# Fused attention and two MoE layers on one core: scores, turning and tails issued in another order, and a four-operation weight decoder

## The chip, the cores and the metric

The kernel runs on one core of a Trainium2 chip. The metric is the device time of one execution in microseconds (us). The engines named here are TensorE (PE in the rows, its weight loads PEld), VectorE (DVE), ScalarE (ACT), GpSimd (POOL) and the queue on SyncE that issues the transfers (SP).

## What is computed

The reference chains three layers over 4 x 576 tokens of width 512:

```python
scores = scale * np.matmul(q, k.transpose(0, 1, 3, 2)) + bias      # 4 batches, 8 heads, 576 x 576
scores = scores - np.max(scores, axis=-1, keepdims=True)
attn = np.exp(scores)
attn = attn / (np.sum(attn, axis=-1, keepdims=True) + 1e-09)
x = matmul(attn, v)                                                # heads joined: 2304 x 512
h = np.maximum(np.maximum(x @ w1, x @ w2), x @ w3)                 # width 768
y = h @ w_out
g = elu(y @ w_in)                                                  # width 2048
out = g @ w_out2
```

The bias depends on the distance of two positions and comes from a small two-layer net. The weights of the two MoE layers come as 64-bit floats.

## The kernel before

**Stages.** From 0 to about 62 us the bias of all heads is computed and written to a scratch array in DRAM. Then comes the attention, up to about 404 us; then the first MoE layer, up to about 713 us, and the second to the end.

**Steps of the attention.** It is cut into 80 steps: 16 groups (one batch and two heads) of five steps, called c0 to c4 here. A step handles 128 query rows of both heads; the last, c4, has 64 rows of both heads in one tile. For step s the program issues:

- *queries times keys* (`unit_qk`, L222): TensorE writes the products of head 0 into the PSUM tile pb0 and those of head 1 into pb1 (c4: pb0 alone).
- *scores* (L230): VectorE adds the bias, writes the tile `e_t` and finds the row's minimum, once for each head. ScalarE then takes the exponential (L235) with the row's sum.
- *reciprocal* (L240, L241) and *diagonal* (L249): one step later VectorE inverts the sums and GpSimd spreads them into a diagonal matrix `dg_t`.
- *turning* (`trans`, L252): two steps later TensorE multiplies `e_t` by that diagonal, which transposes and scales it, into the PSUM tiles tq0 and tq1. `evac` (L295) copies both to SBUF, tq0 by ScalarE, tq1 by VectorE where the step's number is in `EVD` and by ScalarE otherwise.
- *tails* (`tails`, also L252): the last 64 keys are turned into columns of pb0 that the scores don't use (64 to 127 and 832 to 895; the scores use 224 to 799). `evac_tails` (L306) copies them to SBUF with VectorE.
- *values* (`pv`, L319 to L327): TensorE multiplies the turned weights by v into xo0 and xo1. Twice in a group the result is copied out by ScalarE (`x_copy`), summed by VectorE (`x_sum`, L345) and split into a high and a low part by GpSimd.

**What sets the order.** There is no scheduler: every call is entered with a number, the plan is sorted by it, and each engine runs its calls in that order. The numbers are the step plus an offset from the table `OFF`. A call is made to wait for earlier calls on the same PSUM tile; of two calls on pb0 the one that is entered later waits for the one entered sooner.

**Decoder.** Beside the attention, and then beside the first MoE layer, a generator (`decoder`) turns 64-bit weights into 32-bit ones, tile by tile (56 tiles). Each `pump` runs it to its next `yield`. In the attention one pump follows in four of five steps, and a tile takes five pumps. A tile's five VectorE operations stand at L420, L423, L425, L427 and L430, and one ScalarE operation at L422. `split` then makes high and low parts on ScalarE and GpSimd. `fetch` loads the raw tile after the next.

Of the kernel before, what the change touches and what calls it, by code (L numbers as in the profile page):

```python
# [11 lines left out]
F32 = mybir.dt.float32  # L12
F32R = mybir.dt.float32r
I32 = mybir.dt.int32
AF = mybir.ActivationFunctionType
ALU = mybir.AluOpType
# [11 lines left out]
NU = NF // 2  # L28
NB = 384
BIG = 3.0e38  # L30

OFF = {"qk0": 0.0, "qk1": 0.01, "t0": 0.30, "t1": 0.31, "pump": 0.32, "ns": 1.305, "dg": 1.306, "tr": 2.10, "tl": 2.20,
       "evt": 2.311, "ev0": 2.385, "ev1": 2.387, "ex0": 0.38, "ex1": 0.40}
PV_AT = {1: [(4.5, 0), (4.5, 1), (5.5, 2), (5.5, 3), (5.5, 4)],
         4: [(3.5, 0), (3.5, 1), (4.5, 2), (4.5, 3), (5.5, 4)]}
X_AT = {1: 5.6, 4: 5.6}
EVD = {0, 1, 2}  # L40

MOE_LD = 74.39
MOE_AT = [(79.60, 81.00), (80.60, 81.45), (82.00, None)]
# [10 lines left out]
def fused_kernel(ctx, tc, tkq, vv, lt, pk, wm1, wo1, win2, wo2, out):  # L54
    nc = tc.nc
    mm = nc.tensor.matmul

    const = ctx.enter_context(tc.tile_pool(name="const", bufs=1))
# [3 lines left out]
    wpre = wst.enter_context(tc.tile_pool(name="wpre", bufs=1))  # L62

    ident = const.tile([128, 128], F32, name="ident")
    make_identity(nc, ident)
    rebias = const.tile([128, 1], F32, name="rebias")
    nc.vector.memset(rebias, -896.0 * 2.0 ** 23)

    scr = [dram.tile([128 if c < 4 else 64, H, S], F32, name=f"scr{c}") for c in range(5)]

    def hi_of(eng, dst, src):
        if eng == "p":
            nc.gpsimd.tensor_scalar(dst, src, 1.0, 1.0, op0=ALU.mult, op1=ALU.mult)
        elif eng == "a":
            nc.scalar.activation(dst, src, AF.Copy)  # L75
        else:
            nc.vector.tensor_copy(dst, src)  # L77
# [43 lines left out]
    with ExitStack() as pro:  # L121
# [18 lines left out]
        with tc.manual_schedule():  # L140
# [38 lines left out]
            for A in range(36):  # L179
# [15 lines left out]
                c, r = divmod(A, 8)  # L195
# [29 lines left out]
    def scores(s, h):  # L225
        n, c = steps[s]
        if h == 0:
            E[s] = ep.tile([128, 1152], F32, tag="e", name="e_t")
            ST[s] = sp.tile([128, 8], F32, tag="st", name="st_t")
        nc.vector.tensor_tensor_reduce(out=E[s][:, 576 * h:576 * h + 576], in0=PB[h][:, 224:800], in1=BT[n // 4, c, h],  # L230
                                       op0=ALU.add, op1=ALU.min, scale=-0.125, scalar=BIG, accum_out=ST[s][:, h:h + 1])

# [57 lines left out]
    def evac(s, g):  # L290
        n, c = steps[s]
        p = PT[n, c > 1][0]
        if c < 4:
            q0 = 128 * (c % 2) + 64 * g
            hi_of("v" if g and c in EVD else "a", p[:, :, q0:q0 + 64], TQ[g].rearrange("p (k q) -> p k q", k=8))  # L295
        else:
# [58 lines left out]
    DQ = []  # L355
# [4 lines left out]
    RAW = {}  # L360
    n_raw = [0]

    def fetch():
        if n_raw[0] >= len(DQ):
            return
        key = DQ[n_raw[0]]
        n_raw[0] += 1
        r = wpre.tile([128, 512, 2], I32, tag="raw", name="raw", bufs=2)
        src = {"w1": lambda: wm1[key[1], key[2]], "wo": lambda: wo1[key[1]], "wi": lambda: win2[key[1] + NU * key[2]],
               "w3": lambda: wo2[key[1] + NU * key[2]]}[key[0]]()  # L370
        nc.sync.dma_start(r.rearrange("p n t -> p (n t)"), src.bitcast(I32))
        RAW[key] = r
# [7 lines left out]
    def split(key, src, c0=0):  # L380
        direct = key[0] == "w1" and 3 * key[1] + key[2] == WN[0] and WN[0] < WN[1] + 6
        if key[0] == "wo":
            sp2 = WO[0][:, key[1]]
        elif direct:
            sp2 = wr.tile([128, 2, 512], F32R, tag="w", name="w_t")
            WS.append((key, sp2))
            WN[0] += 1
            HERE.add(key)
        else:
            pool, tag = (WPRE2[0], "sp3") if WPRE2 and NSP[0] % 3 == 2 else (wpre, "sp2")  # L390
            sp2 = pool.tile([128, 2, 512], F32R, tag=tag, name=tag, bufs=2 if tag == "sp2" else 1)
            NSP[0] += bool(WPRE2)
        hi, lo, src = sp2[:, 0, c0:], sp2[:, 1, c0:], src[:, c0:]
        parts = [partial(hi_of, "a", hi, src), partial(lo_of, "p", lo, src, hi)]
        if key[0] != "wo":
            parts.append(partial(todo.append, (key, sp2, c0)))
        else:
            SCW[key] = None
        if lim[0] < len(DQ):
            late.extend([parts[0:1], parts[1:3], [store]])  # L400
        else:
            for fn in parts:
                fn()

    def decoder():
        for i, key in enumerate(DQ):
            while i >= lim[0]:
                yield
            if key[0] != "wi":
                dst = wpre.tile([128, 512], F32, tag="t", name="t_w", bufs=2)  # L410
            elif key[2]:
                cw = WPRE2[0].tile([128, 4, 512], F32, tag="cw", name="cw_t", bufs=1)
                dst = cw[:, 3]
            else:
                dst = cw[:, 0]
            t = dst.bitcast(I32)
            r = RAW.pop(key)
            lo, hi = r[:, :, 0], r[:, :, 1]
            x = wpre.tile([128, 512], I32, tag="x", name="x_t", bufs=2)
            nc.vector.tensor_scalar(x, hi, 0x7FF00000, None, op0=ALU.bitwise_and)  # L420
            yield
            nc.scalar.activation(x, x, AF.Relu, bias=rebias, scale=8.0)  # L422
            nc.vector.tensor_scalar(t, hi, 3, 0x7FFFF8, op0=ALU.logical_shift_left, op1=ALU.bitwise_and)  # L423
            yield
            nc.vector.scalar_tensor_tensor(out=t, in0=hi, scalar=-0x80000000, in1=t, op0=ALU.bitwise_and, op1=ALU.bitwise_or)  # L425
            yield
            nc.vector.scalar_tensor_tensor(out=t, in0=lo, scalar=29, in1=t, op0=ALU.logical_shift_right, op1=ALU.bitwise_or)  # L427
            yield
            fetch()
            nc.vector.tensor_tensor(out=t, in0=t, in1=x, op=ALU.bitwise_or)  # L430
            if key[0] != "wi":
                split(key, dst)
            elif key[2] == 0:

                a11, a12, a21, a22 = (cw[:, p, c:c + 256] for p in (0, 3) for c in (0, 256))
                s2, s1, s3, s4 = (cw[:, p, c:c + 256] for p in (1, 2) for c in (0, 256))
                for d, a, b, op in ((s1, a21, a22, ALU.add), (s2, s1, a11, ALU.subtract), (s3, a11, a21, ALU.subtract),
                                    (s4, a12, s2, ALU.subtract)):
                    yield
                    nc.vector.tensor_tensor(out=d, in0=a, in1=b, op=op)  # L440
                for p in range(4):
                    yield
                    if p:
                        yield
                    split(("wi", key[1], p), cw[:, p], 256 if p == 3 and key[1] > 1 else 0)
                    if len(todo) > 1:
                        store()
            yield
            if len(todo) > 1:
                store()  # L450
        while todo:
            store()
# [8 lines left out]
    def store():  # L461
        if not todo:
            return
        key, sp2, c0 = todo.pop(0)
        d = dram.tile([128, 2, 512], F32, name=f"scw_{key[0]}_{key[1]}_{key[2]}")
        nc.sync.dma_start(d[:, :, c0:], sp2.bitcast(F32)[:, :, c0:])
        SCW[key] = d

    dec = decoder()

    def pump(k=1):
# [76 lines left out]
    def at(key, fn, *args):  # L548
        plan.append((key, len(plan), fn, args))

    for s, (n, c) in enumerate(steps):
        o = {nm: s + off for nm, off in OFF.items()}
        at(o["qk0"], unit_qk, s, 0)
        at(o["t0"], scores, s, 0)
        at(o["ex0"], expo, s, 0)
        if c < 4:
            at(o["qk1"], unit_qk, s, 1)
            at(o["t1"], scores, s, 1)
            at(o["ex1"], expo, s, 1)
        at(o["ns"], recip, s)  # L560
        at(o["dg"], diag, s)
        at(o["tr"], trans, s)
        at(o["tl"], tails, s)
        at(o["ev0"], evac, s, 0)
        at(o["ev1"], evac, s, 1)
        at(o["evt"], evac_tails, s)
        if c in (1, 4):
            for off, k in PV_AT[c]:
                at(s + off + 0.01 * k, pv, s, k)
            at(s + X_AT[c], x_copy, s)  # L570
            at(s + X_AT[c] + 0.25, x_sum, s)
            at(s + X_AT[c] + 0.5, x_hi, s)
            at(s + X_AT[c] + 0.75, x_lo, s)
        if s > 5 and c != 1:
            at(o["pump"], pump)
        if n % 4 == 3 and n < 15:
            at(s + 0.45, load_b, n // 4 + 1, c)
# [121 lines left out]
    def small(tag, bufs):  # L699
        return mp.tile([128, NB], F32, tag=tag, name=f"{tag}_t", bufs=bufs)  # L700
# [61 lines left out]
    with tc.manual_schedule():  # L762
        for n, u in enumerate(units + [None]):
# [6 lines left out]
            if n < 2:  # L770

                for i in range(2):
                    w = take_w(("wi", u[1], 3 * i))
                    v = take_w(("w3", pre[1], i)) if pre else None
                    for q, (b, d) in enumerate(((B11, B21), (B12, B22))):
# [3 lines left out]
                        c = small("c", 4)  # L779
# [121 lines left out]
```

## Time and profile before

| | us |
|---|---|
| median of 3 runs (lowest, highest) | 1097.67 (1095.53, 1098.22) |
| the profiled execution's own time | 1097.02 |
| its span, from the first to the last instruction | 1095.2 |
| TensorE busy in the span | 989.3 |
| VectorE busy | 708.7 |
| ScalarE busy | 517.6 |
| GpSimd busy | 339.3 |

The span leaves out 1.8 us of the execution's time. TensorE is busy for 90% of the span, but not evenly: the attention is the stage in which it isn't. The granted TensorE clock was 0.992 of full speed on average.

### The profile page before, as it was taken

What the parts mean: (1) busy time and instruction counts of PE and PEld (TensorE: products, weight loads), DVE (VectorE), ACT (ScalarE), POOL (GpSimd) and SP (SyncE); (2) the same over time, 40 slices, a digit from 0 to 9 for tenths busy, and PEclk for the clock granted to TensorE, in tenths of its full rate; (3) what the DMA queues carried; (4) which work ended last, traced back from release to release, by engine and by line L of the source; (5) the groups of instructions that cost most, each with busy time, mean ns of one, the idle gap of its engine ahead of it and who ended that gap; (6) DMA issues with size and microseconds to landing.
All of it is one profiled execution on the core that took longest, in us unless ns stands there. A gap on an engine that the chain in (4) does not pass through costs nothing.

```text
span 1095.2 us, 28524 instructions
## 1 busy us (share of the span) xinstructions
PE 989.3 (90%) x11748; PEld 846.2 (77%) x11748; DVE 708.7 (65%) x1444; ACT 517.6 (47%) x1071; POOL 339.3 (31%) x419
## 2 busy tenths in 40 slices
PE   7967777777777679999999999999999999999998
PEld 3445555555455468999999999998999889988997
DVE  7946676667666665998878698174567436663333
ACT  8935555555555553333343334163445344444433
POOL 0002323223322233444345345122332323232212
PEclk9979999999999999999999999999999999999999
DMA  7731443343352213567798788325556655575553
GB/s 274 280 122 67 139 144 116 127 142 118 108 172 86 86 58 129 194 221 286 257 350 307 247 293 323 117 97 174 178 192 210 237 176 194 193 253 180 188 194 110
DMA packets 65905, 201.00 MB, mean 184 GB/s; under 512 B 7024, under 2 KB 14832, under 8 KB 65776
## 3 DMA queue, kind: packets, MB, share of 16 engines
q1 hardware_dynamic: 65776, 199.18, 53.0%
q8 instruction: 93, 1.52, 0.5%
q14 instruction: 36, 0.29, 0.1%
HBM read 150.78 MB, written 48.37 MB: 182 GB/s over the span
## 4 chain that ended last, share of the span: by engine, by line
PE 80%; DVE 16%; issue 2%; DMA 1%; ACT 0%; SPq 0%; POOL 0%; DVEq 0%; POOLq 0%; ACTq 0%
PE xo L696 16%; PE pb L740 12%; PE pb L526 11%; DVE e_t L230 9%; PE tq L252 7%; PE tq L740 6%; PE pb L222 5%; PE xo L526 5%; PE tq L526 5%; PE pb L620 3%; DVE p L77 3%; PE pb L183 2%; PE pbb L183 2%; PE xo L620 2%; PE tq L620 2%
## 5 line engine op out<-in xcount | busy, mean ns | idle before, releaser
L81 POOL TENSOR_TENSOR gl<-t_t,gh 128x384 fp32r<-128x384 f32 x96 | 108.8, 1144 | 286.0 <-ACT gh L75 286.0
L235 ACT ACTIVATE e_t<-e_t,st_t 128x576 f32<-128x576 f32 x144 | 111.1, 772 | 164.1 <-DVE st_t L240 155.2
L230 DVE CUSTOM_DVE_ANT_0 e_t<-pb,b_t 128x576 f32<-128x576 f32 x144 | 107.7, 748 | 88.3 <-PE pb L252 67.5
L222 PE MATMUL pb<-kq_t 64*64 64x288 f32 x1152 | 90.9, 425 | 74.0 <-DVE p L77 72.8
L249 POOL TENSOR_SCALAR dg_t<-ident,st_t 128x64 f32<-128x64 f32 x144 | 49.8, 359 | 264.3 <-DVE st_t L241 192.1
L222 PEld LDWEIGHTS pb<-kq_t 64*64 64x64 f32 x1152 | 36.5, 134 | 120.9 <-DVE p L77 105.8
L252 PEld LDWEIGHTS tq<-dg_t,e_t 64*64 64x64 f32 x4608 | 91.0, 139 | 41.0 <-DVE p L77 17.1
L740 PE MATMUL pb<-w_t,gh 128*128 128x512 f32 x384 | 119.3, 392 | 0.0
L526 PE MATMUL pb<-xh,w_t 128*128 128x384 f32 x448 | 116.9, 336 | 0.0
L252 PE MATMUL tq<-dg_t,e_t 64*64 64x64 f32 x4608 | 96.4, 225 | 18.5 <-DVE p L77 12.5
L696 PE MATMUL xo<-tt,w_t 128*128 128x384 f32 x528 | 107.4, 338 | 0.0
L696 PEld LDWEIGHTS xo<-tt,w_t 128*128 128x128 f32 x528 | 95.0, 188 | 7.5
L718 ACT ACTIVATE t_t<-c_t 128x384 f32<-128x384 f32 x96 | 50.0, 521 | 103.7 <-DVE c_t L709 95.5
L696 PE MATMUL xo<-xh,w_t 128*128 128x384 f32 x328 | 94.6, 335 | 0.0
L526 PEld LDWEIGHTS pb<-xh,w_t 128*128 128x128 f32 x448 | 81.2, 188 | 0.5 <-issue 0.4
L319 PE MATMUL xo<-p,tv_t 64*64 64x320 f32 (+1 forms) x1024 | 78.7, 408 | 0.9 <-issue 0.5
L740 PEld LDWEIGHTS pb<-w_t,gh 128*128 128x128 f32 x384 | 70.5, 188 | 6.6
L740 PE MATMUL pb<-w_t,gl 128*128 128x512 f32 x192 | 75.5, 393 | 0.0
L526 PE MATMUL pb<-xl,w_t 128*128 128x384 f32 x224 | 75.3, 336 | 0.0
L75 ACT ACTIVATE gh<-t_t 128x384 fp32r<-128x384 f32 x96 | 48.5, 519 | 33.4 <-DVE t_t L726 33.4
L696 PEld LDWEIGHTS xo<-xh,w_t 128*128 128x128 f32 x328 | 60.2, 188 | 3.0
L726 DVE SCALAR_TENSOR_TENSOR t_t<-t_t,c_t 128x384 f32<-128x384 f32 x96 | 59.0, 632 | 4.5 <-ACT t_t L719 4.1
(131 smaller groups left out, 2198.8 us busy)
## 6 DMA issues: line engine op xcount, KB each, us to landing
w_t<-scw_w SPq DMA_DIRECT2D x90, 512.0 KB, 4.4
w_t<-scw_wi SPq DMA_DIRECT2D x74, 512.0 KB, 3.6
kq_t<-tkq SPq DMA_DIRECT2D x16, 864.0 KB, 5.2
scw_wi<-sp SPq DMA_DIRECT2D x26, 512.0 KB, 4.7
scw_w<-sp SPq DMA_DIRECT2D x22, 512.0 KB, 5.3
raw<-wo SPq DMA_DIRECT2D x22, 512.0 KB, 3.8
scr<-o_t SPq DMA_DIRECT2D x36, 288.0 KB, 3.9
raw<-wm SPq DMA_DIRECT2D x18, 512.0 KB, 3.9
```

The source lines that it names most:

```text
L81: e.tensor_tensor(out=dst, in0=src, in1=hi.bitcast(F32), op=ALU.subtract)
L222: mm(PB[h][H64[g], 224 + 288 * r:512 + 288 * r], t[H64[r], 576 + 576 * a + q0:640 + 576 * a + q0], t[H64[r], 288 * a:288 * a + 288], start ...
L230: nc.vector.tensor_tensor_reduce(out=E[s][:, 576 * h:576 * h + 576], in0=PB[h][:, 224:800], in1=BT[n // 4, c, h], op0=ALU.add, op1=ALU.min ...
L235: nc.scalar.activation(e, e, AF.Exp, bias=st[:, h:h + 1], scale=-1.0, accum_out=st[:, 2 + h:3 + h])
L252: mm(dst, E[s][H64[g], k0:k0 + 64], DG[s][H64[g], h % nheads(s)], start=True, stop=True)
L319: mm(XO[g][H64[h], 0:w], v[H64[g], 128 * k + 64 * h:128 * k + 64 * h + 64], ps[0][H64[g], 4 * h + k, :], start=(k == 0), stop=(k == 3 and ...
L526: mm(ps[blk][:, 0:NB], wt[:, ks], xt[:, kk, t0:t0 + NB], start=(j == 0), stop=(j == 11))
L620: mm(ps[blk][:, 0:NB], WO[0][:, kk, wt, ms], xt[:, bs], start=(j == 0), stop=(j == 3 * NM1 - 1))
L696: mm(ps, w[wt][:, ks], b[xt][:, kk], start=(start and j == 0), stop=(stop and j == 5), skip_group_check=True)
L718: nc.scalar.activation(t, c, AF.Relu, scale=-1.0)
L726: pend.append([lambda: nc.vector.scalar_tensor_tensor(out=t, in0=t, scalar=-1.0, in1=c, op0=ALU.add, op1=ALU.max), last])
L740: mm(acc[t], g[:, ts], w[k], start=(f == 0 and i == 0 and j == 0), stop=(f == NU - 1 and i == 1 and j == 2))
```

## The change

Four edits. The offsets of the scores (`t0`, `t1`), of the reciprocal (`ns`) and of the diagonal (`dg`) put the scores of a step ahead of the turning and the tails that share the step, instead of behind them. `x_sum` is entered later, which puts it behind the first scores of the following step. Step c1 leaves `EVD`, so that the copy of its tq1 is ScalarE's. The decoder takes the magnitude of the high word with one ScalarE operation a tile ahead, clamps it, and needs four VectorE operations in place of five.

```diff
-OFF = {"qk0": 0.0, "qk1": 0.01, "t0": 0.30, "t1": 0.31, "pump": 0.32, "ns": 1.305, "dg": 1.306, "tr": 2.10, "tl": 2.20,
-       "evt": 2.311, "ev0": 2.385, "ev1": 2.387, "ex0": 0.38, "ex1": 0.40}
+LEAST, MOST = (float(np.array(b, np.uint32).view(np.float32)) for b in (896 << 20, 0x47EFFFFF))
+OFF = {"qk0": 0.0, "qk1": 0.01, "t0": 0.02, "ns": 1.025, "dg": 1.026, "t1": 0.03, "tr": 2.10, "tl": 2.20, "evt": 2.311,
+       "pump": 0.32, "ev0": 2.385, "ev1": 2.387, "ex0": 0.38, "ex1": 0.40}
...
-EVD = {0, 1, 2}
+EVD = {0, 2}
...
-    rebias = const.tile([128, 1], F32, name="rebias")
-    nc.vector.memset(rebias, -896.0 * 2.0 ** 23)
...
+    MAG = {}
+
+    def magnitude(i):
+        if i < len(DQ):
+            MAG[i] = wpre.tile([128, 512], F32, tag="x", name="x_t", bufs=2)
+            nc.scalar.activation(MAG[i], RAW[DQ[i]][:, :, 1].bitcast(F32), AF.Abs)
+
     def decoder():
+        magnitude(0)
...
-            x = wpre.tile([128, 512], I32, tag="x", name="x_t", bufs=2)
-            nc.vector.tensor_scalar(x, hi, 0x7FF00000, None, op0=ALU.bitwise_and)
+            x = MAG.pop(i)
+            nc.vector.tensor_scalar(x, x, LEAST, MOST, op0=ALU.max, op1=ALU.min)
             yield
-            nc.scalar.activation(x, x, AF.Relu, bias=rebias, scale=8.0)
-            nc.vector.tensor_scalar(t, hi, 3, 0x7FFFF8, op0=ALU.logical_shift_left, op1=ALU.bitwise_and)
+            nc.vector.tensor_scalar(t, x.bitcast(I32), 3, 0x3FFFFFF8, op0=ALU.logical_shift_left, op1=ALU.bitwise_and)
             yield
-            nc.vector.scalar_tensor_tensor(out=t, in0=hi, scalar=-0x80000000, in1=t, op0=ALU.bitwise_and, op1=ALU.bitwise_or)
+            nc.vector.scalar_tensor_tensor(out=t, in0=hi, scalar=-0x40000000, in1=t, op0=ALU.bitwise_and, op1=ALU.bitwise_or)
+            magnitude(i + 1)
             yield
             nc.vector.scalar_tensor_tensor(out=t, in0=lo, scalar=29, in1=t, op0=ALU.logical_shift_right, op1=ALU.bitwise_or)
             yield
             fetch()
-            nc.vector.tensor_tensor(out=t, in0=t, in1=x, op=ALU.bitwise_or)
...
-            at(s + X_AT[c] + 0.25, x_sum, s)
+            at(s + X_AT[c] + 0.427, x_sum, s)
```

The line numbers of the changed kernel are one to eleven off those of the kernel before. On TensorE and in the queue of SyncE every instruction keeps its place in the row. What TensorE's instructions wait for changes. The first place is TensorE at the end of a step, before: the last turning, the tails into pb0 (named pb_99), the values, and the products of the next step. What an instruction waits for stands in brackets, by the engine whose count it watches.

```order
L252 MATMUL tq_860<-dg_t,e_t 64x64 x2
L252 MATMUL pb_99<-dg_t,e_t 64x64 x4
L319 MATMUL xo_861<-p_1029,tv_t 64x320 [waits Activation_49]
L319 MATMUL xo_861<-p_1029,tv_t 64x320
L319 MATMUL xo_862<-p_1029,tv_t 64x320 [waits DVE_49]
L319 MATMUL xo_862<-p_1029,tv_t 64x320
L319 MATMUL xo_861<-p_1029,tv_t 64x320 x2
L319 MATMUL xo_862<-p_1029,tv_t 64x320 x2
L222 MATMUL pb_99<-kq_t 64x288 [waits DVE_49]
```

And now, at the same place (pb0 is pb_97 here):

```order
L251 MATMUL tq_858<-dg_t,e_t 64x64 x2
L251 MATMUL pb_97<-dg_t,e_t 64x64 [waits DVE_49]
L251 MATMUL pb_97<-dg_t,e_t 64x64 x3
L318 MATMUL xo_859<-p_1035,tv_t 64x320 [waits Activation_49]
L318 MATMUL xo_859<-p_1035,tv_t 64x320
L318 MATMUL xo_860<-p_1035,tv_t 64x320 [waits DVE_49]
L318 MATMUL xo_860<-p_1035,tv_t 64x320
L318 MATMUL xo_859<-p_1035,tv_t 64x320 x2
L318 MATMUL xo_860<-p_1035,tv_t 64x320 x2
L221 MATMUL pb_97<-kq_t 64x288 [waits DVE_49]
```

The order of these instructions is the same. The first of the tails now waits for VectorE, namely for the scores of head 0 of the step, which it did not before; the products of the next step wait for VectorE (the copy of the tails) in both.

The second place is VectorE over one step of the attention, before: the copy of a c4 step's tails, `x_sum`, the scores of head 0 (pb_99), the reciprocal of the step before, the scores of head 1 (pb_100), and the copy of the tails.

```order
L77 COPY p_1154<-pb_99 64x128
L345 TENSOR_TENSOR xf<-xo_862,xf 128x256 [waits PE_49,Activation_49]
L230 ISA e_t,st_t<-pb_99,b_t 128x576 [waits PE_49]
L230 ISA st_t 128x1
L240 TENSOR_SCALAR st_t<-st_t 128x2
L241 RECIPROCAL st_t<-st_t 128x2 [waits DVE_49]
L230 ISA e_t,st_t<-pb_100,b_t 128x576
L230 ISA st_t 128x1
L77 COPY p_1212<-pb_99 128x128
```

And now:

```order
L76 COPY p_1161<-pb_97 64x128 [waits PE_49]
L229 ISA e_t,st_t<-pb_97,b_t 128x576 [waits PE_49]
L229 ISA st_t 128x1
L239 TENSOR_SCALAR st_t<-st_t 128x2 [waits Activation_49]
L240 RECIPROCAL st_t<-st_t 128x2 [waits DVE_49]
L344 TENSOR_TENSOR xf<-xo_860,xf 128x256 [waits Activation_49]
L229 ISA e_t,st_t<-pb_98,b_t 128x576 [waits PE_49]
L229 ISA st_t 128x1
L76 COPY p_1219<-pb_97 128x128 [waits PE_49]
```

`x_sum` has moved from ahead of the scores to between the two scores. The wait of head 0's scores for TensorE was one for the last of the tails and is one for the products of their own head; head 1's scores, which had no wait of their own, wait for their products; and the copy of the tails, which had none, waits for the tails.

## Rows read from the trace of the kernel before

**Rows 1.** Busy time of each engine by stage: stretch, its length, busy us (instructions).
```profile
84.00:404.00 320.00, 236.92 (x6973) 166.24 (x6967) 215.89 (x617) 174.86 (x423) 94.64 (x201) 0.99 0.34 114
500.00:713.00 213.00, 213.00 (x1231) 212.99 (x1230) 158.37 (x244) 76.22 (x145) 87.56 (x69) 1.00 0.75 267
```

**Rows 2.** Who waited for whom, 62 to 404 us: total us, times, longest.
```profile
PE pb L222 <- DVE p L77: 72.8, 76, 2.0
DVE e_t L230 <- PE pb L252: 67.5, 63, 3.6
...
PEld tq L252 <- POOL dg_t L249: 9.1, 15, 4.2
```

**Rows 3.** Timeline of one c2 step: start, us, engine, line; last, the idle time before.
```profile
87.55 0.69 PEld L222 LDWEIGHTS pb<-kq_t 64*64 64x64 f32 x16 [1.17 <-DVE p L77]
...
88.33 1.21 PEld L252 LDWEIGHTS tq<-dg_t,e_t 64*64 64x64 f32 x64
...
88.92 0.42 DVE L345 TENSOR_TENSOR xf<-xo,xf 128x256 f32<-128x256 f32 x1 [1.43 <-ACT xf L341]
...
89.50 0.30 PE L252 MATMUL pb<-dg_t,e_t 64*64 64x64 f32 x8
89.56 0.75 PEld L319 LDWEIGHTS xo<-p,tv_t 64*64 64x64 f32 x16
...
89.86 0.76 DVE L230 CUSTOM_DVE_ANT_0 e_t<-pb,b_t 128x576 f32<-128x576 f32 x1 [0.52 <-PE pb L252]
...
91.49 0.29 DVE L77 COPY p<-pb 128x128 f32<-128x128 f32 x1
...
91.83 0.69 PEld L222 LDWEIGHTS pb<-kq_t 64*64 64x64 f32 x16 [1.52 <-DVE p L77]
```

**Rows 4.** Timeline: other steps' first weight loads of the products (c0, c1, c4, c0, c0).
```profile
79.41 0.69 PEld L222 LDWEIGHTS pb<-kq_t 64*64 64x64 f32 x16 [1.54 <-DVE p L77]
...
83.77 0.69 PEld L222 LDWEIGHTS pb<-kq_t 64*64 64x64 f32 x16 [1.60 <-DVE p L77]
...
96.73 0.21 PEld L222 LDWEIGHTS pb<-kq_t 64*64 64x64 f32 x8 [1.60 <-DVE p L77]
...
100.38 0.69 PEld L222 LDWEIGHTS pb<-kq_t 64*64 64x64 f32 x16 [1.15 <-DVE p L77]
...
383.70 0.69 PEld L222 LDWEIGHTS pb<-kq_t 64*64 64x64 f32 x16 [1.03 <-DVE p L77]
```

**Rows 5.** Timeline of a c3 and a c4 step, 265 to 272 us.
```profile
265.07 0.95 PEld L252 LDWEIGHTS tq<-dg_t,e_t 64*64 64x64 f32 x58 [0.58 <-DVE p L77]
...
266.38 0.76 DVE L230 CUSTOM_DVE_ANT_0 e_t<-pb,b_t 128x576 f32<-128x576 f32 x1 [1.37 <-PE pb L252]
...
268.35 0.72 PE L222 MATMUL pb<-kq_t 64*64 64x288 f32 x8 [0.94 <-DVE p L77]
...
270.86 0.76 DVE L230 CUSTOM_DVE_ANT_0 e_t<-pb,b_t 128x576 f32<-128x576 f32 x1 [1.37 <-PE xo L327]
...
271.82 0.27 DVE L77 COPY p<-pb 128x128 f32<-128x128 f32 x1
```

**Rows 6.** Groups of instructions by shape: count, busy us, mean ns, idle before.
```profile
L425 DVE SCALAR_TENSOR_TENSOR t_w<-raw,t_w 128x512 int32<-128x512 int32 x40 | 44.3, 1108 | 0.8
...
L427 DVE SCALAR_TENSOR_TENSOR t_w<-raw,t_w 128x512 int32<-128x512 int32 x40 | 37.1, 928 | 0.6
...
L77 DVE COPY p<-tq 128x512 f32<-128x512 f32 x48 | 32.7, 682 | 0.0
```

**Rows 7.** One line's instructions (duration ns, least/median/most), and the raw tiles' landing.
```profile
L420 DVE TENSOR_SCALAR x_t<-raw x56: 407/419/1236, 91.7 to 677.8; 128x512 int32<-128x512 int32 x56
...
DMA to landing us min/median/max: 3.1/4.0/10.8
```

**Rows 8.** Transfers (count, KB each, median us from issue to landing).
```profile
raw<-win SPq DMA_DIRECT2D x16, 512.0 KB, 5.7
```

**Rows 9.** The chain that ended last (start, us, what), one unit of the first MoE layer.
```profile
438.48 4.16 PE tq L526 x24
```

## The prediction

> **What bounds the kernel now.** I read the stages first. In the first MoE layer TensorE is busy for all of its 213 us; in the attention it is busy for 236.92 us of 320 in the 75 steps from 84 us on, while VectorE is busy for 215.89 and ScalarE for 174.86 [rows 1]. So no engine is full there, and something makes them take turns. The list of waits says what: TensorE's products waited 72.8 us in 76 waits for VectorE's copy of the tails, and VectorE's scores waited 67.5 us in 63 waits for TensorE's tails [rows 2]. That is a ring, and one step shows it whole [rows 3]. In that c2 step the products begin at 87.55 us, the turning 0.78 us later, the tails' last product ends at 89.80, and only then, at 89.86, do the scores of this step begin, though their own products were long done. The two scores with the reciprocal between them take 1.63 us to the copy of the tails at 91.49, and 0.34 us after that copy began the next products start. The sum, 0.78 + 1.53 + 1.63 + 0.34 = 4.28 us, is the step. TensorE stands still while VectorE does the scores, and VectorE while TensorE turns.
>
> The other steps [rows 3, 4]: c0 takes 4.36 us (79.41 to 83.77), c1 3.78, c2 4.28, c3 4.90 and c4 3.65 (96.73 to 100.38), a round of 20.97 us. From 79.41 to 383.70 us there are 14 rounds, 21.74 us on average: several are longer by stops that wait for nothing the profile names, and by the decoder.
>
> **What the change does to the ring.** It moves no instruction of TensorE. The scores are entered ahead of the tails, so they wait for their own products alone, and the tails wait for the scores of head 0. The products of one head take 0.72 us when they stand alone, in a c4 step [rows 5]; with 0.06 us from one engine to the next the scores can begin 0.78 us after the products do, as soon as the turning. They then run beside it. The ring that is left is products, scores, copy of the tails, products: 0.78 + 1.63 + 0.34 = 2.75 us. The turning and the tails, 0.78 + 1.47 = 2.25 us to the tails' end by the c2 step [rows 3], are done before VectorE comes to their copy 2.41 us in, and so are hidden; TensorE does the values in the time that it used to wait.
>
> What lies on this ring now and did not before:
>
> - *x_sum.* It ran in a gap in which VectorE waited for the tails (0.42 us, after 1.43 us of idle time) [rows 3]. Now it stands between the two scores of c0 and c2, and adds 0.42 us to each. The transfer of its result is GpSimd's and isn't waited for.
> - *The decoder and the copy of tq1.* After the copy of the tails VectorE does a decoder operation and, in c2 and c4, the copy of tq1 (0.68 us [rows 6]). Until now they ran while the products and the turning did. If the copy of the tails starts at time t, the next scores could start at t + 0.34 + 0.78, and VectorE is free at t + 0.20 + p + 0.65, where p is the decoder's operation: late by p - 0.27. The new decoder has two tensor_scalar operations; the nearest is the old first one, 0.41 us alone and up to 1.24 [rows 7], and I take 0.41. The two scalar_tensor_tensor operations stay, 1.11 and 0.93 us [rows 6]. One pump in five has no VectorE operation left. The delays are 0.14, 0.14, 0.84, 0.66 and 0, 0.36 us on average, and they fall on the steps behind c2 and c4, which are c3 and c0. The least is 0 and the most 0.97 (every operation at 1.24).
> - *The copy of tq1 of c1* goes to ScalarE, behind one exponential and the copy of tq0. By my count it ends some 0.7 us into the c4 step; the turning there starts at 0.78 us, and takes 1.31 us to the tails' end, as in the c3 step where it also came late [rows 5]. So c4 takes 0.78 + 1.31 + 0.34 = 2.43 us, more than its ring (0.78 + 0.96, from scores to copy [rows 5], + 0.34 = 2.08).
>
> The steps become: c0 2.75 + 0.42 + 0.36 = 3.53, c1 2.75, c2 3.17, c3 3.11 and c4 2.43 us, a round of 14.99. To this I add the wait for GpSimd's diagonal, which isn't touched: 9.1 us in 15 waits, 0.6 us a round [rows 2]. That makes 15.6 us.
>
> Is TensorE able to do that? By the c2 step it issues its last weight load 2.01 + 0.75 = 2.76 us after the first [rows 3], and c2 is one of the fullest: five such steps are 13.8 us, below 15.6. By busy time it would be tight: 236.92 us over 75 steps is 3.16 us a step, 15.8 a round [rows 1]. [...]
>
> **The rest of the change.** The decoder does 56 tiles, most of them beside the MoE layer, where TensorE has no idle time to give back (213.00 us busy of 213 [rows 1]): the VectorE time saved there is worth nothing. ScalarE keeps one operation for each tile. The copy that leaves VectorE saves it 0.68 us a round and its lateness behind c3. The removed constant is nothing.
>
> **The sum.** 20.97 - 15.6 = 5.4 us by the round shown; 21.74 - 15.6 = 6.1 by the mean, part of which are stops that stay. I take 5.7. There are 15 rounds and two full steps ahead of them: 15.4 rounds, 88 us. The profiled execution took 1097.02 us, its span 1095.2 and 1.8 around it, and is 0.65 us from the median of the runs, 1097.67. So 1097.0 - 88 = **1009 us**.
>
> **Rivals.**
>
> - *VectorE becomes the bound of the round.* If every decoder operation meets GpSimd and takes the 1.24 us of [rows 7], c3 and c0 lose 0.61 us more each; with x_sum kept waiting by ScalarE's copy for as long as its own 0.42 us in two steps, the round is 15.6 + 1.2 + 0.8 = 17.6. The saving is 3.4 to 4.1, 3.8 a round, and the time 1097 - 58 = 1039 us. For it: VectorE is already the fuller of the two vector engines [rows 1]. Against: the decoder gets shorter.
> - *TensorE's pace alone is the bound*: the round is 13.8 us, the saving 7.5 and the time 1097 - 115 = 982 us. It would need the delays above to be absorbed from step to step; c0 and c2 speak against it with 3.17 us of ring each.
> - *The wait is turned round and nothing is won.* The tails now wait for VectorE as the scores did for TensorE. Should VectorE come to the scores of head 0 as late as the turning's end (more than 1.5 us late in every step, where I count 0.36 in two of five), the step is what it was: 1097 us. [...]
> - *Slower: ScalarE waits for raw weights in the first MoE layer.* The magnitude of the next tile is entered at the third pump after the transfer for it was, and five pumps make one unit of 4.16 us [rows 9], so the data has 2.5 us. It lands in 4.0 us in the median [rows 7], in 5.7 for the 16 tiles of the second layer's first weights [rows 8]. Before, VectorE waited for it with a whole tile's time more in hand. ScalarE would stand 1.5 us for 28 tiles and 3.2 us for 16, 93 us, with the copies out of PSUM queued behind. If all of that reached TensorE, 1009 + 93 = 1102 us, slower by 0.4%; it decides from 2.0 us a tile on the path (88 / 44). Against it: four pairs of PSUM tiles turn there, so that a copy may be three units of 4.16 us late, and ScalarE is busy for 76 us of 213 [rows 1].
>
> **Chances.** The forecast 0.72, its own range 998 to 1026; VectorE as the bound 0.13; TensorE's pace 0.06; turned round 0.04; slower 0.05. A difference under 0.3% can't be told from no change here. The range from 998 to 1040 leaves out the TensorE case, the last two and some of the second: about 0.2. Faster by over 0.3% has the first three, 0.91; within 0.3% 0.04; slower 0.05.
>
> **What would show it.** Right: the wait of the scores for the tails gone from the list of waits (67.5 us) and replaced by short waits for the products; the products' wait for the copy of the tails under 25 us of 72.8; first weight loads of a round 15 to 16 us apart, c0 the longest step and c4 the shortest; the attention ending near 317 us; the MoE stages as long as before. Wrong: a long wait of TensorE's tails for the scores; waits of the raw tiles on ScalarE with TensorE idle past the attention; rounds above 17 us.

## The result and the profile after

The changed kernel takes 1019.77 us (median of 4 runs, 1019.40 to 1023.16), beside 1097.16 (4 runs, 1095.53 to 1098.22) for the kernel before: a ratio of 0.930, 95% interval 0.928 to 0.933. The forecast was 1009 us, with a range from 998 to 1040. The profiled execution took 1020.0 us, with a span of 1018.1.

From the pages of the kernel after and, in the second fence, of the kernel before, the busy times and the chain of work that ended last, by engine:

```profile
PE 982.6 (97%) x11748; PEld 874.9 (86%) x11748; DVE 650.5 (64%) x1371; ACT 522.5 (51%) x1087; POOL 335.3 (33%) x419
...
PE 92%; DVE 5%; issue 2%; DMA 1%; ACT 0%; SPq 0%; POOL 0%; DVEq 0%; POOLq 0%; ACTq 0%
```

```profile
PE 80%; DVE 16%; issue 2%; DMA 1%; ACT 0%; SPq 0%; POOL 0%; DVEq 0%; POOLq 0%; ACTq 0%
```

TensorE's busy time hardly changed (989.3 us before, 982.6 after); its share rose because the span fell. The chain that ran back and forth between TensorE and VectorE is now almost all TensorE's. The same by stage (stretch, its length, busy us of PE, PEld, DVE, ACT and POOL with their instructions, granted clock, DMA share, GB/s):

```profile
84.00:327.00 243.00, 225.91 (x6896) 190.62 (x6892) 188.72 (x587) 179.47 (x428) 95.55 (x201) 0.99 0.45 153
...
423.00:636.00 213.00, 213.00 (x1215) 213.00 (x1214) 130.89 (x207) 69.83 (x139) 80.84 (x65) 1.00 0.71 250
636.00:1018.00 382.00, 377.41 (x1872) 339.68 (x1870) 193.78 (x310) 170.67 (x342) 108.45 (x96) 1.00 0.56 185
```

In the attention TensorE is busy for 93% of the time, where it was 74% [rows 1]. The waits of that stretch, 62 to 327 us (who waited for whom: us in total, times, longest):

```profile
DVE e_t L229 <- PE pb L221: 39.4, 47, 1.8
...
DVE p L76 <- PE pb L251: 13.3, 25, 3.0
...
PEld tq L251 <- issue: 9.6, 13, 2.0
...
PEld pb L221 <- DVE p L76: 4.2, 13, 0.6
...
PEld pb L251 <- DVE st_t L229: 3.2, 8, 1.3
...
PE pb L221 <- DVE p L76: 1.3, 3, 0.4
```

In the kernel before, from 62 to 404 us, the weight loads of the products waited:

```profile
PEld pb L222 <- DVE p L77: 105.8, 77, 2.2
```

The scores (L229) no longer wait for the tails, 67.5 us in [rows 2], but for their own products, 39.4 us. The products' wait for the copy of the tails fell from 105.8 us to 4.2 on the weight loads, and from 72.8 [rows 2] to 1.3 on the matmuls. The wait turned the other way, tails (pb, L251) for the scores, is 3.2 us in all.

The ring of one c2 step and of the c3 and c4 steps behind it, to set beside [rows 3] (start, us, engine, line, operation; in brackets the idle time before):

```profile
231.25 0.94 PEld L221 LDWEIGHTS pb<-kq_t 64*64 64x64 f32 x16
...
232.06 1.43 PEld L251 LDWEIGHTS tq<-dg_t,e_t 64*64 64x64 f32 x64
...
232.30 0.76 DVE L229 CUSTOM_DVE_ANT_0 e_t<-pb,b_t 128x576 f32<-128x576 f32 x1 [1.11 <-PE pb L221]
...
233.47 0.98 PEld L318 LDWEIGHTS xo<-p,tv_t 64*64 64x64 f32 x16
...
234.26 0.28 DVE L76 COPY p<-pb 128x128 f32<-128x128 f32 x1
...
234.45 1.28 POOL L80 TENSOR_TENSOR sp<-t_w,sp 128x512 fp32r<-128x512 f32 x1
234.46 1.55 DVE L429 TENSOR_SCALAR t_w<-x_t 128x512 int32<-128x512 int32 x1
234.59 0.88 PEld L221 LDWEIGHTS pb<-kq_t 64*64 64x64 f32 x16
...
236.67 0.95 PEld L251 LDWEIGHTS tq<-dg_t,e_t 64*64 64x64 f32 x58 [0.90 <-DVE p L76]
...
238.49 0.50 PEld L221 LDWEIGHTS pb<-kq_t 64*64 64x64 f32 x8
...
241.14 0.45 PEld L221 LDWEIGHTS pb<-kq_t 64*64 64x64 f32 x12
```

The c2 step takes 3.34 us (231.25 to 234.59) in place of 4.28. Two things fill it at once: the products, scores and copy of the tails (1.05 + 1.96 + 0.33 us), and TensorE's own row of weight loads, which runs from 231.25 to 234.45 with hardly a gap. The experiments below tell them apart.

First and last full round, by the first weight load of c0's products (separate answers of the timeline):

```profile
74.17 0.45 PEld L221 LDWEIGHTS pb<-kq_t 64*64 64x64 f32 x12 [0.55 <-DVE p L76]
...
303.20 0.21 PEld L221 LDWEIGHTS pb<-kq_t 64*64 64x64 f32 x8
```

14 rounds in 229.03 us are 16.36 us each, beside 21.74. The first units of the first MoE layer begin at 320.76 us in place of 404.43: the attention gave 83.7 us. From there to the end the kernel before takes 690.8 us (1095.2 - 404.43) and the changed one 697.3 (1018.1 - 320.76). So 6.6 us were given back in stages that the forecast had left as they were.

### The profile page after: what moved, and what is told of

The parts are those of the page before. It is cut to its first block, busy times and chain, and to the rows that moved or that the text cites. A ratio compares the mean times of both kernels' runs of the same rounds, so it can differ in the third digit from the quotient of the medians.

```text
span 1018.1 us, 28497 instructions
## 1 busy us (share of the span) xinstructions
PE 982.6 (97%) x11748; PEld 874.9 (86%) x11748; DVE 650.5 (64%) x1371; ACT 522.5 (51%) x1087; POOL 335.3 (33%) x419
## 4 chain that ended last, share of the span: by engine, by line
PE 92%; DVE 5%; issue 2%; DMA 1%; ACT 0%; SPq 0%; POOL 0%; DVEq 0%; POOLq 0%; ACTq 0%
PE xo L702 18%; PE pb L746 13%; PE pb L532 12%; PE tq L746 6%; PE tq L251 6%; PE xo L318 6%; PE xo L532 5%; PE tq L532 5%; PE pb L221 5%; PE pb L626 4%; PE pb L182 3%; PE pbb L182 2%; PE tq L626 2%; PE xo L626 2%; DVE e_t L229 2%
## 5 line engine op out<-in xcount | busy, mean ns | idle before, releaser
L80 POOL TENSOR_TENSOR gl<-t_t,gh 128x384 fp32r<-128x384 f32 x96 | 108.5, 1141 | 288.7 <-ACT gh L74 288.7
L229 DVE CUSTOM_DVE_ANT_0 e_t<-pb,b_t 128x576 f32<-128x576 f32 x144 | 107.8, 750 | 39.7 <-PE pb L221 39.6
L248 POOL TENSOR_SCALAR dg_t<-ident,st_t 128x64 f32<-128x64 f32 x144 | 47.2, 341 | 218.1 <-DVE st_t L240 96.3
L251 PEld LDWEIGHTS tq<-dg_t,e_t 64*64 64x64 f32 x4608 | 96.0, 136 | 26.8 <-issue 9.9
L251 PE MATMUL tq<-dg_t,e_t 64*64 64x64 f32 x4608 | 97.2, 222 | 14.6 <-issue 7.4
L221 PE MATMUL pb<-kq_t 64*64 64x288 f32 x1152 | 99.3, 417 | 3.3 <-DVE p L76 1.3
L318 PE MATMUL xo<-p,tv_t 64*64 64x320 f32 (+1 forms) x1024 | 84.6, 409 | 0.8 <-issue 0.5
L409 ACT ACTIVATE x_t<-raw 128x512 f32<-128x512 f32 x56 | 37.7, 674 | 91.4 <-DMA raw<-win 44.8
L74 ACT ACTIVATE p<-tq 128x512 f32<-128x512 f32 (+1 forms) x128 | 62.9, 529 | 16.4 <-PE tq L251 15.6
L221 PEld LDWEIGHTS pb<-kq_t 64*64 64x64 f32 x1152 | 51.3, 134 | 22.5 <-DVE p L76 4.2
```

The source lines that it names most:

```text
L80: e.tensor_tensor(out=dst, in0=src, in1=hi.bitcast(F32), op=ALU.subtract)
L221: mm(PB[h][H64[g], 224 + 288 * r:512 + 288 * r], t[H64[r], 576 + 576 * a + q0:640 + 576 * a + q0], t[H64[r], 288 * a:288 * a + 288], start ...
L251: mm(dst, E[s][H64[g], k0:k0 + 64], DG[s][H64[g], h % nheads(s)], start=True, stop=True)
L318: mm(XO[g][H64[h], 0:w], v[H64[g], 128 * k + 64 * h:128 * k + 64 * h + 64], ps[0][H64[g], 4 * h + k, :], start=(k == 0), stop=(k == 3 and ...
```

## Experiments

Theory: the gain is the ring products, tails, scores, copy of the tails, cut open by entering the scores ahead of the tails; the decoder is beside the path. Rivals: TensorE's or VectorE's pace alone sets the round; the decoder does part of it; the turning's place, and not the tails', matters. Each ratio is to the kernel before on the same chip, with its 95% interval.

**The new order alone**, in the kernel before.

```diff
-OFF = {"qk0": 0.0, "qk1": 0.01, "t0": 0.30, "t1": 0.31, "pump": 0.32, "ns": 1.305, "dg": 1.306, "tr": 2.10, "tl": 2.20,
-       "evt": 2.311, "ev0": 2.385, "ev1": 2.387, "ex0": 0.38, "ex1": 0.40}
+OFF = {"qk0": 0.0, "qk1": 0.01, "t0": 0.02, "ns": 1.025, "dg": 1.026, "t1": 0.03, "tr": 2.10, "tl": 2.20, "evt": 2.311,
+       "pump": 0.32, "ev0": 2.385, "ev1": 2.387, "ex0": 0.38, "ex1": 0.40}
```

> The kernel before with the new table of offsets alone: the old decoder, the old place of x_sum and the old three copies of tq1 on VectorE stay. Theory (the order of the scores against the tails is the whole gain, and TensorE's own pace is what is left): 1020 to 1035 us; x_sum at its old place, behind the copy of tq1, may hold VectorE back a little at c0 and c2. Rival (the shorter decoder and the other edits give a good part, since VectorE bounds the round): 1050 to 1075 us.

Measured: 1022.88 us (1019.36 to 1024.26), ratio 0.931 (0.928 to 0.933). As the theory had it, nearly the whole result comes from the table. Its list of waits from 62 to 327 us has one that the changed kernel has not (L341 is ScalarE's copy of the values):

```profile
DVE xf L345 <- ACT xf L341: 20.3, 15, 1.4
```

That is `x_sum`, ahead of the scores, waiting for ScalarE.

**The new decoder alone**, in the kernel before: the edit is the decoder's part of the diff shown with the change.

> The kernel before with the new decoder alone. Theory (VectorE's decoder work lies off the ring of the old order, beside the products and the turning, and TensorE is full in the MoE layers): 1092 to 1098 us. Rival (VectorE's load counts): 1070 to 1085 us, some 0.5 us in each of 60 pumps.

Measured: 1097.72 us (1093.22 to 1100.07, 10 runs), ratio 0.999 (0.998 to 1.001). Worth nothing as a whole. But its profiled run ends the attention at 400.68 us, 3.75 earlier than before, and takes 697.4 us from there (span 1098.1), 6.6 more: the loss behind the attention belongs to this part of the change.

**Scores between turning and tails.** Old kernel; the scores stand behind the turning of the step, but still ahead of the tails.

```diff
-... "t0": 0.30, "t1": 0.31, "pump": 0.32, "ns": 1.305, "dg": 1.306, ...
+... "t0": 0.15, "t1": 0.154, "pump": 0.32, "ns": 1.152, "dg": 1.153, ...
```

> The kernel before with the scores, the reciprocal and the diagonal entered between the turning and the tails: behind the turning as before, ahead of the tails as in the changed kernel. Theory (it is the wait on the tails, which write the tile that the scores read, and not the turning): within 5 us of the run with the new order alone. Rival (it is the place ahead of the turning that counts): 1085 to 1100 us.

Measured: 1022.92 us (1022.09 to 1024.60), ratio 0.932 (0.929 to 0.934), the same as the new table. This is less of a test than it looks. The turning writes tq0 and tq1, which the scores don't touch, so the place of the scores ahead of it or behind it makes no wait: as built, TensorE, VectorE, ScalarE and SyncE have the same instructions in the same order in both programs, each waiting for the same engines, and only GpSimd has another order. The run shows that GpSimd's order is worth nothing here (1022.92 beside 1022.88 us). That the tails held the scores is read from the wait in [rows 2], which names the tails as what ended it and is gone after the change, and from the tile pb0, which both use.

**The changed kernel with the old decoder**, its bias constant included.

> The changed kernel with the old decoder: five VectorE operations for each tile. Theory (TensorE's pace bounds the round, VectorE has some room): 1020 to 1028 us. Rival (VectorE bounds the round): 1035 to 1050 us, some 0.4 us in each of 60 pumps.

Measured: 1011.96 us (1008.75 to 1014.82), ratio 0.921 (0.918 to 0.924): 8 us faster than the change as made. No theory had this. The attention ends at 319.30 us, 1.5 earlier; the rest takes 691.3 us, as in the kernel before.

**VectorE work added to the ring**: one memset of 128x512 in each step, between the scores and the copy of the tails, in the changed kernel and in the kernel before.

```diff
+    idle = const.tile([128, 512], F32, name="idle")
...
+        at(s + 0.031, nc.vector.memset, idle, 0.0)
```

(0.3105 in the kernel before.)

> The changed kernel with a VectorE memset of 128 x 512 (some 0.5 us) added in each of the 80 steps between the scores and the copy of the tails. Theory (TensorE's pace bounds the steps now, and the ring through VectorE has room): 1022 to 1035 us. Rival (the ring through VectorE is the bound, as the prediction's steps had it): 1050 to 1062 us, 80 x 0.5 = 40 us more.

> The kernel before with the same memset at the same place. Theory (scores, copy of the tails and products are on its ring): 1130 to 1140 us, 80 x 0.5 = 40 us more. Rival (VectorE has idle time there that takes it up): 1097 to 1105 us.

Measured: a memset takes 485 ns, 38.8 us for all 80. The kernel before becomes 1127.78 us (1125.05 to 1129.40), ratio 1.027 (1.024 to 1.030): 30 us, a little under the range expected, but far above the rival's. In its trace, from 62 to 435 us, the weight loads of the products wait 142.7 us for the copy of the tails, 36.9 more than before, nearly all of the added work; in turn those of the turning wait 8.4 us for the copies out of PSUM in place of 17.1. So VectorE's work between the scores and the copy was on the ring. The changed kernel becomes 1029.09 us (1027.56 to 1031.54), ratio 0.938 (0.935 to 0.942): 9 us, as the theory had it. Its waits from 62 to 327 us, and one of its c2 steps:

```profile
PEld pb L222 <- DVE p L77: 37.4, 72, 1.0
```

```profile
113.44 0.69 PEld L222 LDWEIGHTS pb<-kq_t 64*64 64x64 f32 x16 [0.45 <-DVE p L77]
...
114.23 0.76 DVE L230 CUSTOM_DVE_ANT_0 e_t<-pb,b_t 128x576 f32<-128x576 f32 x1 [0.84 <-PE pb L222]
...
116.72 0.23 DVE L77 COPY p<-pb 128x128 f32<-128x128 f32 x1
...
117.00 0.69 PEld L222 LDWEIGHTS pb<-kq_t 64*64 64x64 f32 x16 [0.63 <-DVE p L77]
```

The products wait again in nearly every step, 0.5 us in the mean, so the ring sets the pace here. Behind such a gap the scores begin 0.79 us after the products, and c2 takes 3.56 us; without the memset its ring would be 3.08. In the changed kernel c2 takes 3.34, with the scores 1.05 us after the products: there TensorE's full row sets the step, and the ring has some 0.26 us to spare.

**TensorE work taken out**: the values of the fourth block of keys (k = 3) are left out, so the output lacks these keys; the scores and all the rest stay. In the changed kernel and in the kernel before.

```diff
-                at(s + off + 0.01 * k, pv, s, k)
+                if k != 3:
+                    at(s + off + 0.01 * k, pv, s, k)
```

> The changed kernel without the fourth 128 keys in the product with the values: TensorE does 16 of its instructions with 256 or 320 columns less in each c1 and c3 step together, some 0.35 + 0.43 us of issue in a round. Its output lacks these keys. Theory (TensorE's pace bounds): 16 x 0.78 = 12 us less, 1005 to 1011 us. Rival (the ring through VectorE bounds): 1016 to 1021 us.

> The kernel before without the fourth 128 keys in the product with the values; its output lacks them. Theory (in the old order the values are done while TensorE waits for the scores and the copy of the tails, so they are off its ring): 1094 to 1098 us. Rival: 1083 to 1088 us.

Measured: the kernel before 1098.52 us (1094.98 to 1101.96), ratio 1.001 (0.999 to 1.002), half a us above the range of the theory and 10 above that of the rival: the values lay in TensorE's idle time. The changed kernel 1018.41 us (1016.34 to 1022.21), ratio 0.928 (0.925 to 0.931), 1.4 us below the change and within the spread: the rival's range, and far from the 12 us that TensorE's pace as the only bound would give. Waits from 62 to 327 us of this run, and one of its c2 steps:

```profile
PEld tq L251 <- issue: 15.3, 24, 2.3
...
PEld pb L221 <- DVE p L76: 15.1, 34, 0.8
```

```profile
145.72 0.69 PEld L221 LDWEIGHTS pb<-kq_t 64*64 64x64 f32 x16 [0.40 <-DVE p L76]
...
146.50 0.76 DVE L229 CUSTOM_DVE_ANT_0 e_t<-pb,b_t 128x576 f32<-128x576 f32 x1 [0.84 <-PE pb L221]
...
148.46 0.28 DVE L76 COPY p<-pb 128x128 f32<-128x128 f32 x1
...
148.80 0.88 PEld L221 LDWEIGHTS pb<-kq_t 64*64 64x64 f32 x16
```

The time taken from TensorE came back as waits for the copy of the tails (4.2 to 15.1 us) and as stops of the turning that the profile gives no reason for (9.6 to 15.3). The values left out belong to c1 and c3. Typical steps of these two keep their length (2.99 and 3.02 us), with a wait for the copy at their end in place of the work, so the ring is as long as TensorE's row there. c2 and c4, whose products now begin behind that gap, fall from 3.34 to 3.08 us and from 2.65 to about 2.44. So this run and the one with added VectorE work agree: ring and TensorE's row lie within 0.3 us of each other in each of these steps, and neither is the only bound.

**The constant.** The units of the first MoE layer are 24 products that stream xh and xl past weight tiles w_t. In the chain that ended last they take 4.16 us before [rows 9] and 4.24 after, while the units of its second part (L626) take 6.24 in both. From the chain of the kernel after and, in the second fence, of the kernel before (start, us, what):

```profile
320.76 4.43 PE pb L532 x24
...
355.24 4.24 PE tq L532 x24
...
425.09 6.24 PE tq L626 x36
```

```profile
507.14 6.24 PE tq L620 x36
```

All four kernels with the new decoder that had run by then had 4.24, and all that kept the old one 4.16. The new decoder needs no bias constant, a tile of 128x1 allocated ahead of the weights. As the programs are built, the first w_t tile starts at byte 17,056 of a partition with it (4 bytes a partition, for which 32 are set aside) and 17,024 without; xh, allocated from the other end, stays at 155,360. Products that stream hh past wo_t, which both moved, kept their time, 6.24 us a unit. Two edits put the old distance back without touching the decoder: a spare constant in the old place, or a spare tile behind xh and xl, which moves these down by 32 bytes.

```diff
     make_identity(nc, ident)
+    spare = const.tile([128, 1], F32, name="spare")
+    nc.vector.memset(spare, 0.0)
```

> After, with one spare constant of 128x1 allocated where the old bias constant stood and read by nothing, so that the weight tiles w_t lie 32 bytes higher, as before the change, with the new decoder as it is. Theory 'addresses': the 2% on the products from xh and xl come from where the weight tiles lie, so the units of 24 products go back from 4.24 to 4.16 us and the whole to about 1013 us (1009 to 1015). Rival 'decoder': the new decoder's own work (its operation on ScalarE, the wider VectorE operations) slows TensorE; units stay at 4.24 us and the time at 1020 us (1018 to 1023).

```diff
     nc.vector.tensor_copy(ident2[64:128], ident[64:128, 64:128])
+    spare = xp.tile([128, 1], F32, name="spare")
+    nc.vector.memset(spare, 0.0)
```

> After, with the spare 128x1 tile at the end of the pool of xh and xl instead: the weight tiles stay where they are after the change, xh and xl lie 32 bytes lower. If the distance of a product's two operands is what counts (modulo 64 bytes: moe1_out, whose two operands both moved by 32 bytes, kept its 6.24 us), the units go back to 4.16 us and the time to about 1013 us. If the place of the weights alone counts, or the new decoder does it, units stay at 4.24 us and the time at 1020 us.

Measured: 1009.96 us (1008.87 to 1010.12), ratio 0.920 (0.918 to 0.921), and 1010.92 us (1009.64 to 1012.21), ratio 0.921 (0.919 to 0.922). From the chains of the two, and then from the groups of instructions of the second layer in the kernel after and in that with the spare constant (busy us, mean ns of one):

```profile
317.21 4.36 PE pb L534 x24
...
372.05 4.16 PE xo L534 x24
```

```profile
319.43 4.37 PE pb L534 x24
...
374.27 4.16 PE xo L534 x24
```

```profile
L702 PE MATMUL xo<-tt,w_t 128*128 128x384 f32 x528 | 107.4, 338 | 0.0
L702 PE MATMUL xo<-xh,w_t 128*128 128x384 f32 x328 | 95.9, 339 | 0.0
```

```profile
L704 PE MATMUL xo<-tt,w_t 128*128 128x384 f32 x528 | 107.4, 338 | 0.0
L704 PE MATMUL xo<-xh,w_t 128*128 128x384 f32 x328 | 94.6, 335 | 0.0
```

Both took the time that the theory of addresses gave, or a little less. The new decoder is innocent: what slows the products is where their two operands lie to each other. Both edits also add a memset, but so does the run with added VectorE work, whose tile of 2,048 bytes moves w_t by a multiple of 64, and its units stay at 4.24 us. 54 units at 0.08 us are 4.3 us, and the second layer's products from xh and xl some 2 more, about the 6.6 us given back; with either spare tile the stages behind the attention take 690.8 us again (1008.0 - 317.21, 1010.2 - 319.43). The median gains 8.9 to 9.8 us. The attention of the profiled executions ended at 317.21 and 319.43 us in place of 320.76, but these are single executions, and those of the changed kernel alone lie 3.8 us apart: whether the place of the tiles matters in the attention too isn't shown. The kernel with the spare constant has the lowest median of the study, by less than its neighbours' spread.

**Old decoder, and tq1 of c1 back on VectorE**, which splits the 11 us between the table alone (1022.88) and the kernel with the old decoder (1011.96).

```diff
-EVD = {0, 2}
+EVD = {0, 1, 2}
```

> The order, x_sum's new place and the old decoder, as in the run that took 1011.96 us, but with the copies of tq1 for c1 back on VectorE (EVD 0, 1, 2). It splits the 11 us between the new order alone (1022.88 us) and that run. By the prediction's ring the copy of 682 ns back on c1 lengthens that step alone, by up to 0.68 of a round: up to 10 us, so 1018 to 1023 us. Rival: x_sum's place gave the 11 us, and the copies' engine next to nothing: 1011 to 1014 us.

Measured: 1018.73 us (1014.35 to 1019.03), ratio 0.927 (0.924 to 0.929). The move of `x_sum` behind the reciprocal gave about 4 us of the 11, and the copy on ScalarE about 7. The attention of the profiled runs ends at 331.57 (table alone), 325.91 (`x_sum` too) and 319.30 us (copy too), the same order in larger steps. The intervals of the first two ratios overlap a little, so the 4 is a weak figure. 1018.73 lies in the range that the prediction's ring gave.

**The decoder's piece behind the copy of tq1**, in the kernel with the spare constant.

```diff
-       "pump": 0.32, "ev0": 2.385, "ev1": 2.387, ...
+       "pump": 0.39, "ev0": 2.385, "ev1": 2.387, ...
```

> The kernel of the spare constant, with the decoder's piece after the copy of tq1 and not before it (pump 0.39 for 0.32). If the decoder's piece ahead of the copy makes the scores of c3 and c0 late on the ring (0.36 us a round by the prediction, 15.4 rounds: 5 us), it is 4 to 6 us faster than the run with the spare constant alone, near 1008 us. If TensorE's own pace sets the round, within 2 us of it.

Measured: 1010.38 us (1008.46 to 1013.38), ratio 0.921 (0.918 to 0.923): nothing, as a pace set by TensorE would have it. The lateness that I put on the ring for the decoder's piece isn't there to be won back this way.

## Why the prediction was right, and where it was off

**The ring** was the right cause. The table alone gave 75 us of the 77, the added VectorE work showed VectorE on the ring before (30 of 38.8 us in the time, 36.9 in the products' waits), and the values left out showed these off it. That the tails were the link to cut is read from the scores' wait, 67.5 us before and gone after. Of what the prediction said would show it, the scores' wait for the tails is gone, the products' wait for the copy is well below 25 us, and c4 is the shortest step. Rounds of 16.36 us in the mean are just above its 15 to 16, and five of the 14 are above the 17 that was to mean wrong (17.03 to 19.39 us), with stops or a late c3 step in them. c0 is not clearly the longest step: without a stop it takes 3.13 to 3.40 us, c2 3.29 to 3.46. The MoE stages are 6.6 us longer than before.

**The step that was wrong** is one sentence: "The removed constant is nothing." It cost 6.6 us behind the attention; by the medians 8.9 to 9.8 us in all. With the constant's place kept the kernel takes 1009.96 us, the attention ends at 317.21 us ("near 317") and the MoE stages are as long as before. So the sum came out right for the work that was changed, and wrong for the tiles that were shifted by 32 bytes. That it came out within 1 us owes something to luck, since its terms erred in both directions (below).

**The account by parts**, from the experiments: the table 75 us, `x_sum` behind the reciprocal 4, the copy of c1's tq1 on ScalarE 7, the new decoder 2 (1011.96 to 1009.96, within the runs' spread), and the shifted tiles -10: 78, beside 77 measured. These are steps of one chain of runs from the kernel before to the kernel after, so that they add up proves nothing. The decoder was forecast to be worth nothing and is worth nothing that can be told; the copy that left VectorE was priced at its lateness behind c3, and its 7 us are 0.44 us a round of the copy's 0.68.

**Sizes within the sum.** c2 was put at 3.17 us and took 3.34: the scores begin 1.05 us after the products do and not 0.78, as the products no longer stand alone but follow the values of the step before without a gap. Where they do stand behind a gap, in the run with fewer values, it is 0.78 and c2 takes 3.08. c1 took some 3.0 in place of 2.75, c4 2.65 in place of 2.43, c3 about 3.03 in place of 3.11, and 3.90 in the c3 step shown above, behind L429. Typical steps come to 15.2 to 15.4 us a round, beside 14.99 in the sum. The decoder's pieces were mis-sized in both directions: L431 and L434, put at 1.11 and 0.93 us, take 0.68 in the median within the attention, and L429, put at 0.41, takes 1.18. The 0.6 us added for the diagonal had another form: that wait is one of 5.2 us now, and instead TensorE's weight loads of turning, tails and products stood still for 15 us in all with no reason in the profile (8 before). The attention gave 83.7 us of the 88.

**TensorE's pace** was put too low, at 13.8 us a round, and with it the argument that TensorE would not set any step. I had taken it from weight loads of the c2 step that had idle time between them; in an unbroken row the 64 of the turning take 1.43 us, not 1.21 [rows 3], and the 16 of the values 0.98, not 0.75. The stages once more, of the kernel after and within the attention (columns as above):

```profile
84.00:300.00 216.00, 201.03 (x6223) 169.38 (x6218) 169.08 (x529) 161.92 (x386) 85.84 (x181) 0.99 0.48 163
```

At 16.36 us a round these 216 us are 66 steps, so matmuls are busy for 3.05 us a step, 15.2 a round. That is close to the 15.8 that the prediction had from busy time, beside the 15.6 of its sum. The weight loads are busy for 169.38 of the 216 us, matmuls for 201.03; the run with added VectorE work and the one with fewer values show TensorE's row and the ring within some 0.3 us a step of each other.

**The rivals.** VectorE as the bound at 17.6 us a round: not reached, though what it rested on is seen: L429 takes 1.18 us in the median. In its seven cases of 1.18 us and more GpSimd's split (L80) runs beside it for 0.9 us or longer, and L429 ends 0.28 to 0.30 us after the split does; the other six take 0.42 to 0.43. The spread over one window of the kernel after (ns, least/median/most, 84 to 327 us):

```profile
L427 DVE TENSOR_SCALAR x_t<-x_t x12: 410/417/990, 102.2 to 314.7; 128x512 f32<-128x512 f32 x12
...
L429 DVE TENSOR_SCALAR t_w<-x_t x13: 416/1183/1557, 86.1 to 315.2; 128x512 int32<-128x512 int32 x13
```

I had taken 0.41 us for both. TensorE's pace alone: refuted as the only bound by the values left out, though it sets c2 and c4. The wait turned round: 3.2 us, refuted. Slower by raw weights: its total was met and its path was wrong. The waits of the whole execution:

```profile
ACT x_t L409 <- DMA raw<-win: 44.8, 15, 7.3
ACT x_t L409 <- DMA raw<-wo: 31.3, 11, 4.2
ACT x_t L409 <- DMA raw<-wm: 15.4, 6, 3.2
```

ScalarE stood 91.5 us for raw tiles, where the rival said 93; the nearness is in part luck, as there were 32 waits of 2.9 us in the mean and not 28 of 1.5 and 16 of 3.2. TensorE was still busy for 213.00 us of the 213 of the first layer's stretch. That fits the argument against that rival, the four pairs of PSUM tiles; no run tried fewer.

## What to carry to other kernels

Where two engines take turns on one tile, look for the consumer that is entered behind an unrelated writer of the same tile: moving that one entry was worth 75 us here, beside 72.8 of waiting, and what is left of the ring lies within some 0.3 us a step of TensorE's own unbroken row, which has to be read from a stretch without gaps (1.43 us for 64 weight loads, where 1.21 was taken). An edit that adds or removes even a tile of 4 bytes a partition can shift every tile allocated behind it, by 32 bytes here, so compare the mean time of instructions that the change doesn't touch; a spare tile is a cheap test. A long wait in the list, such as 91 us of ScalarE, need not cost anything: look at whether the engine behind it stays busy, as TensorE did for 213.00 us of 213.

## What the runs showed of the hardware

The time of a product depended on where its two SBUF operands lie to each other: with the first w_t tile and xh 138,304 bytes apart a unit of 24 takes 4.16 us, with 138,336 bytes 4.24, whichever of the two was moved, at a granted clock of 1.00. In the run with added VectorE work they are 136,288 bytes apart, 2,048 less, and a unit takes 4.24. The difference is 2%; where in the chip it arises, no run shows. What the rule is behind the distances stays open: products that stream tt past w_t, a pair whose distance was the same in both layouts, take 338 ns in both, and as built that distance is a multiple of 64 bytes just as 138,304 is, so that alone isn't the rule.

TensorE's stops for no reason that the profile shows grew as its gaps were closed, from 8 us of the attention to 15; they were 21 with the values left out, and 4.5 with VectorE work added, which opens gaps again (weight loads of turning, tails and products, summed). What they are wasn't tried.
